# Issuing a tuned attention and highway-FFN kernel in the order of a list schedule, with PSUM banks moved from scores to transposes and PV

## The chip, the cores and the metric

One core of one Trainium2 chip. The metric is device microseconds of one launch (median of the runs). The kernel before was timed at 243.35 us in three runs ahead of the prediction. Ratios are the mean time of one kernel's fast runs over the mean of the other's fast runs of the same rounds, so they are not quite the ratio of the medians quoted beside them. A run more than 1.5% above the fastest of its kernel is called slow and is left out of them.

## The reference

Sliding-window attention with a linear (ALiBi) bias, then one highway layer over all tokens. Sizes: 8 batches, 8 heads, 576 positions, head width 64, window 128, model width 512; float32 in and out.

```
scores = q @ k.T / 8 - slope[h] * |i - j|        where 0 <= i - j < 128, else -1e9
attn   = softmax(scores);  x = attn @ v           # x as (8 * 576, 512)
H = relu(x @ w_h);  T = sigmoid(x @ w_t + b_t)
out = T * H + (1 - T) * x
```

## The kernel before

Batches are handled in four *pairs*. A pair has two row stages of eight heads, so the program has 64 *units* (pair, stage, head). A unit is: scores on TensorE (PE; its weight loads are shown apart, as PEld), exponential on ScalarE (ACT), mask multiply on VectorE (DVE), PV matmuls (`attn @ v`) on PE, and normalisation on DVE. A pair's q and k are first transposed on PE, ten groups a pair, each copied out of PSUM, the memory that TensorE writes to, by DVE or ACT. After eight units their 512-wide rows go through the FFN in four or five *blocks*: transpose, H and T matmuls, tanh on ACT, then `0.5*tanh + 0.5` on GpSimd (POOL; I call this the gate arithmetic), the gate multiply on DVE, the output add on POOL, and a store issued by SyncE. All loads of q, k, v and weights are issued by POOL and convert float32 to bfloat16 on the way; the last 64 of the 576 positions of q and k come by loads of their own, the *tail loads*.

In the traces of this case an engine does not pass an instruction that has to wait (VectorE stood 11.36 us at one, below), so the order of the program counts. It is emitted by a hand-written loop:

```python
ps_sc = ...(name="ps_sc", bufs=2)   # a score buffer holds 128x1024 float32
ps_tr = ...(bufs=1); ps_av = ...(bufs=1); ps_a = ...(bufs=1); ps_z = ...(bufs=1)
...
for u in range(NU + 2):
    m, s, h = unit(u)
    if u < NU:
        if u < len(first): transposes(0, *first[u])      # pair 0
        soft(u)                                          # exponential of unit u
        ...                                              # loads of pair m + 1 at r = u % 16 < 9
        if u + 1 < NU: scores(u + 1)                     # straight behind it
    if 1 <= u <= NU: mask(u - 1)
    ...                                                  # half of this slot's FFN steps
    if 2 <= u:
        pv(u - 2); norm(u - 2)
    ...                                                  # the other half
    if u < NU and m + 1 < ND:
        r = u % (2 * H)
        if r >= 5 and r - 5 < len(TRS):
            transposes(m + 1, *TRS[r - 5])               # next pair, from unit 5 on
```

The bias of T is added by a matmul of one row: `nc.tensor.matmul(out=pz, lhsT=ones1, rhs=bT, ...)` with `ones1` of 1x128 and `bT` of 1x512.

The softmax here doesn't subtract the row's maximum and nothing guards it: scores larger than these inputs give would overflow.

## Time and profile before

| part of the span | from, to (us) | length |
|---|---|---|
| start of the program to unit 0's exponential | 0 to 10.7 | 10.7 |
| units 0 to 15 | 10.7 to 73.7 | 63.0 |
| units 16 to 31 (pair 1) | 73.7 to 125.1 | 51.4 |
| units 32 to 47 (pair 2) | 125.1 to 179.1 | 54.0 |
| units 48 to 63 (pair 3, up to the last exponential) | 179.1 to 216.8 | 37.7 |
| tail | 216.8 to 245.3 | 28.5 |

How to read it: the start of each unit's exponential is a mile post that every version of the kernel has, so stages of two versions can be laid side by side. The lines behind the table are in the prediction. FFN work of one stage runs beside the units of later stages, so a stage's length also depends on how much FFN work was put off into it. The profiled run took 247.06 us, 2.0% above the fastest of this kernel (242.29) and so slow by the rule above: the stages together are some 4 us longer here than in a fast run, and a difference of 1 us in one of them says nothing.

### The profile page before, as it was taken

Reading aid. Unit: us, or ns where it says so; the run is one execution under the profiler, and the core shown is the slowest. Engines: PE = TensorE matmul, PEld = TensorE weight load, DVE = VectorE, ACT = ScalarE, POOL = GpSimd, SP = SyncE. Lnnn points to the kernel's source line nnn. Section 1 sums busy time; section 2 is a strip of 40 time slices with the busy share of each in tenths; the row PEclk is TensorE's granted clock in tenths of the full one; section 3 lists DMA queues with packets and bytes.
Section 4 is the critical chain, followed back from the end, with each engine's and each line's share of the span. In section 5 each row is a group of like instructions: output and inputs, shape, how many; then the busy total and the mean of one; then the engine's idle time right before and its main releaser. Section 6 shows DMA issues by size and latency. Waiting matters only on the chain.

```text
span 245.3 us, 5032 instructions
## 1 busy us (share of the span) xinstructions
PE 177.5 (72%) x2004; PEld 96.5 (39%) x2004; DVE 142.1 (58%) x339; ACT 126.3 (51%) x157; POOL 119.1 (49%) x139
## 2 busy tenths in 40 slices
PE   1355702498898777868887986888887997887980
PEld 1133402376553334445533343455443344533430
DVE  4169501364677656565786575365786586785340
ACT  2324610185665756447675645646656766562440
POOL 8987733300245876531257784412233356223572
PEclk9999965556999999799999798879999999999996
DMA  5999999995019999930159999530113223122243
GB/s 61 135 191 190 167 129 198 143 108 12 6 41 157 217 199 163 104 73 17 45 81 217 208 155 127 67 74 0 45 43 77 54 56 78 43 63 69 52 112 92
DMA packets 70199, 24.97 MB, mean 102 GB/s; under 512 B 48160, under 2 KB 65568, under 8 KB 70176
## 3 DMA queue, kind: packets, MB, share of 16 engines
q0 software_dynamic: 63392, 15.21, 80.5%
q1 hardware_dynamic: 6784, 9.45, 15.3%
q8 instruction: 15, 0.25, 0.4%
q14 instruction: 8, 0.07, 0.1%
HBM read 30.41 MB, written 9.44 MB: 162 GB/s over the span
## 4 chain that ended last, share of the span: by engine, by line
POOL 34%; issue 25%; DMA 16%; DVE 9%; PE 8%; ACT 3%; SPq 2%; POOLq 1%; ACTq 0%
POOL ot L368 16%; DMA kl<-in_k_dram 8%; POOL tt L359 8%; DMA out_dram<-ot 5%; DVE uu L364 5%; POOL va L102 4%; DMA ql<-in_q_dram 3%; PE pt L197 3%; SPq L380 2%; PE av L290 2%; DVE m L167 1%; POOL ktl L93 1%; PE sc L254 1%; ACT xt L332 1%; POOL kl L73 1%
## 5 line engine op out<-in xcount | busy, mean ns | idle before, releaser
L264 ACT ACTIVATE pt<-sc,bias 128x1024 bf16<-128x1024 f32 x64 | 71.0, 1118 | 0.7 <-PE sc L254 0.7
L359 POOL TENSOR_SCALAR tt<-tt 128x512 f16<-128x512 f16 x36 | 22.2, 618 | 85.8 <-ACT tt L358 77.7
L368 POOL TENSOR_TENSOR ot<-uu,x 128x512 f32<-128x512 bf16 x36 | 44.5, 1235 | 19.6 <-DVE uu L364 16.3
L273 DVE TENSOR_TENSOR pt<-pt,m 128x1024 bf16<-128x1024 bf16 x64 | 52.2, 816 | 0.0
L364 DVE TENSOR_TENSOR uu<-uu,tt 128x512 bf16<-128x512 bf16 x36 | 15.3, 426 | 52.4 <-POOL tt L359 52.4
L290 PE MATMUL av<-va,pt 128*128 128x65 bf16 (+1 forms) x576 | 32.7, 205 | 13.8 <-DVE x L316 12.1
L358 ACT ACTIVATE tt<-pz 128x512 f16<-128x512 f32 x36 | 21.5, 597 | 39.3 <-PE pz L355 38.1
L340 PE MATMUL pa<-wH,xt 128*128 128x512 bf16 x144 | 39.8, 401 | 1.3 <-ACT xt L332 0.8
L353 PE MATMUL pz<-wT,xt 128*128 128x512 bf16 x144 | 38.9, 394 | 0.0
L290 PEld LDWEIGHTS <-pt 128*128 128x128 bf16 (+1 forms) x576 | 24.7, 105 | 33.7 <-DVE x L316 22.2
L332 ACT COPY xt<-pt 128x512 bf16<-128x512 bf16 x36 | 21.1, 586 | 31.2 <-PE pt L326 31.0
L209 ACT COPY kt<-pt 128x1024 bf16<-128x1024 bf16 x16 | 16.2, 1012 | 39.4 <-PE pt L197 39.4
L254 PE MATMUL sc<-qt,kt 64*128 64x256 bf16 (+2 forms) x384 | 29.6, 260 | 7.2 <-ACT kt L209 4.4
L316 DVE TENSOR_TENSOR x<-av,rd 128x256 bf16<-128x256 f32 (+1 forms) x64 | 29.3, 458 | 6.0 <-POOL ot L368 3.8
L197 PE MATMUL pt<-ident,ql 128*64 128x128 bf16 x256 | 13.3, 255 | 22.5 <-DMA ql<-in_q_dram 13.4
L102 POOL DMA_DIRECT2D va<-in_v_dram x20 | 22.2, 1113 | 12.6 <-DMA kl<-in_k_dram 4.5
L344 DVE SCALAR_TENSOR_TENSOR uu<-pa,x 128x512 bf16<-128x512 f32 x36 | 24.6, 682 | 5.3 <-PE pa L340 5.3
L326 PE MATMUL pt<-ident,x 128*128 128x128 bf16 x144 | 15.2, 228 | 8.4 <-DVE qt L204 4.2
L254 PEld LDWEIGHTS <-kt 64*128 64x128 bf16 x384 | 14.8, 100 | 15.9 <-issue 6.4
L197 PEld LDWEIGHTS <-ql 128*64 128x64 bf16 x256 | 10.6, 131 | 25.4 <-DMA ql<-in_q_dram 19.2
L204 DVE COPY qt<-pt 128x1024 bf16<-128x1024 bf16 x16 | 11.0, 689 | 15.2 <-PE pt L197 15.2
L340 PEld LDWEIGHTS <-xt 128*128 128x128 bf16 x144 | 11.7, 100 | 15.4 <-issue 4.5
(45 smaller groups left out, 129.1 us busy)
## 6 DMA issues: line engine op xcount, KB each, us to landing
out_dram<-ot SPq DMA_DIRECT2D x128, 64.0 KB, 1.7
va<-in_v_dram POOLq DMA_DIRECT2D x16, 256.0 KB, 8.7
ql<-in_q_dram POOLq DMA_DIRECT2D x3, 1024.0 KB, 11.1
kl<-in_k_dram POOLq DMA_DIRECT2D x3, 1024.0 KB, 12.3
out_dram<-ot SPq DMA_DIRECT2D x8, 128.0 KB, 2.4
ql<-in_q_dram POOLq DMA_DIRECT2D x4, 128.0 KB, 4.8
kl<-in_k_dram POOLq DMA_DIRECT2D x4, 128.0 KB, 5.3
ql<-in_q_dram POOLq DMA_DIRECT2D x2, 256.0 KB, 7.2
```

Of the source, the lines that this page charges most:

```text
L102: nc.gpsimd.dma_start(out=VA[i][0:n, c, :, :, 0:D].rearrange("s r h d -> s (r h) d"), in_=v[2 * m : 2 * m + 2, :, c * P : c * P + n, :].re ...
L197: nc.tensor.transpose(out=pt[r * D : (r + 1) * D, hl * 512 + t * P : hl * 512 + (t + 1) * P], in_=L[:, r, 2 * hp + hl, t * D : (t + 1) * D ...
L254: nc.tensor.matmul(out=sc[:, r, off : off + w], lhsT=KT[i][rows, h, j * P : (j + 1) * P], rhs=rhs, start=True, stop=True,)
L264: nc.scalar.activation(out=pt[:], in_=SC.pop(u)[:], func=ACTF.Exp, bias=BIAS[:, h : h + 1], scale=scale,)
L273: nc.vector.tensor_tensor(out=pt[:], in0=pt[:], in1=mk.to_broadcast([P, 2, 512]), op=ALU.mult,)
L290: nc.tensor.matmul(out=av[rows, g, :], lhsT=pt[:, r, off : off + w], rhs=va[:, j, r, h, :], start=n == 0, stop=n == len(terms) - 1,)
L316: nc.vector.tensor_tensor(out=x[:, 0:nb, h * D : (h + 1) * D], in0=av[:, 0:nb, 0:D], in1=rd[:, 0:nb].to_broadcast([P, nb, D]), op=ALU.mult,)
L340: nc.tensor.matmul(out=pa[:], lhsT=xt[:, c, :], rhs=wH[:, c, :], start=c == 0, stop=c == NCK - 1)
L353: nc.tensor.matmul(out=pz[:], lhsT=xt[:, c, :], rhs=wT[:, c, :], start=c == 0, stop=False)
L359: nc.gpsimd.tensor_scalar(out=tt[:], in0=tt[:], scalar1=0.5, scalar2=0.5, op0=ALU.mult, op1=ALU.add)
L364: nc.vector.tensor_tensor(out=uu[:], in0=uu[:], in1=TT.pop((st, b))[:], op=ALU.mult)
L368: nc.gpsimd.tensor_tensor(out=ot[:], in0=UU.pop((st, b))[:], in1=X[st][:, b, :], op=ALU.add)
```

## The change

Its intent: no hand-placed order. The builder makes a graph of pieces (each with an engine, an estimated cost, a priority, what it depends on, and which PSUM buffers it takes and frees), simulates the engines greedily, and emits the pieces in the order of their simulated start. Beside that, PSUM goes from two score buffers to one, which makes room for a second transpose and a second PV buffer (a *bank* below). The first loads are cut in two instead of three parts; the mask tables are halved and built with five broadcast instructions instead of 37; four k copies of pair 0 go from ScalarE to VectorE; some other buffers grow. The diff, cut to its core (`# ...` marks cuts):

```diff
-    ps_sc = ...bufs=2; ps_tr = ...bufs=1; ps_av = ...bufs=1; ps_a, ps_z = ...bufs=1
+    RING = {"sc": 1, "tr": 2, "av": 2, "a": 1, "z": 1}
-    p0 bufs=11, p1 bufs=4, x bufs=2, ot in ft (bufs=3)
+    p0 bufs=12, p1 bufs=5, x bufs=3, ot bufs=4
-    load_qk(0, slice(0, 2)); # ... load_qk(0, slice(2, 4)); load_qk(0, slice(4, 8))
+    # slice(0, 2), then slice(2, 8), q and k apart
-    M0, M1: 5 copies and 32 tensor_scalar of 128x128 or 128x64
+    def c_mask(s):  # copies, and tensor_tensor with a broadcast per-head column
+    # evac/f_xe/f_u/f_th/f_t/f_st: each copy or follow-up is now a piece of its own
-    for u in range(NU + 2): # ... the hand-written loop
+    node("ident", "POOL", 600, -90, c_ident)
+    # ...
+    def ld(key, prio, nbytes, emit, deps=(), cost=850):
+        node(key, "POOL", cost, prio, emit, deps, land=nbytes)
+    # ...
+    ld(("qk", m, w, 0), tl + w * T, qk_b, ..., [("tr", m - 2, w, hp) for hp in range(4)], cost=1200)
+    node(("qkm", u), "PE", (330, 360)[s], tu - 1.3 * T, ..., need, take=["sc"])
+    node(("exp", u), "ACT", 1118, tu - 1.2 * T, ..., [("qkm", u), "cbias"], free=["sc"])
+    node(("z", kb), "PE", 1090, t + 0.5 * dt, ..., take=["z"])
+    node(("t", kb), "POOL", 630, t + 0.6 * dt, lambda kb=kb: f_t(*kb), [("th", kb)])
+    # ...
+    while todo:
+        # per engine: candidates with the earliest possible start; within LOOK = 100 ns the
+        # lowest priority number; of all engines the one that starts first
+        # ...
+        if land:                      # a load
+            dma = max(dma, t + cost) + land / RATE      # 370 bytes a ns
+            when[key] = dma + LAND                      # 2000 ns
+    order.sort(key=lambda o: o[0])
+    for t, key in order:
+        nodes[key][3]()
```

## The prediction

> **What bounds the kernel now.** I read in this order: the page's busy shares and slices, the table of stages, the timeline where TensorE is empty, the waits, the chain, the groups. First the slices of the page, 40 over the span.
>
> ```profile
> PE   1355702498898777868887986888887997887980
> DVE  4169501364677656565786575365786586785340
> ACT  2324610185665756447675645646656766562440
> PEclk9999965556999999799999798879999999999996
> DMA  5999999995019999930159999530113223122243
> ```
>
> TensorE (PE) is the busiest engine, but there is a hole in slices 5 to 7, near 30 to 50 us, while the DMA row is full and PEclk has fallen to half. Afterwards PE sits at seven to nine tenths, no engine at ten.
>
> I cut the span where the softmax exponentials (64 "units": 4 batch pairs x 2 row stages x 8 heads) start: unit 0 at 10.7 us, unit 7 at 49.5, unit 16 at 73.7, unit 32 at 125.1, unit 48 at 179.1, the last at 216.8. The table of windows, with columns as headed:
>
> ```profile
> core 0: us, PE busy (x) PEld busy (x) DVE busy (x) ACT busy (x) POOL busy (x), PEclk, DMA share, GB/s
> 10.70:30.50 19.80, 11.37 (x144) 7.38 (x144) 13.05 (x53) 8.88 (x9) 15.86 (x23) 1.00 1.74 183
> 30.50:49.50 19.00, 4.58 (x66) 3.44 (x64) 3.44 (x8) 2.85 (x5) 6.08 (x6) 0.55 2.44 155
> 49.50:73.70 24.20, 22.05 (x308) 14.65 (x309) 15.62 (x33) 16.27 (x21) 4.50 (x5) 0.79 1.21 41
> 73.70:125.10 51.40, 41.11 (x503) 22.20 (x502) 33.75 (x72) 31.11 (x40) 27.21 (x30) 0.97 0.94 117
> 125.10:179.10 54.00, 44.17 (x503) 23.07 (x502) 33.80 (x72) 31.24 (x41) 26.21 (x29) 0.91 0.89 111
> 179.10:216.80 37.70, 32.24 (x330) 15.61 (x328) 26.82 (x62) 24.89 (x33) 15.64 (x16) 1.00 0.26 63
> 216.80:245.30 28.50, 18.67 (x123) 8.09 (x122) 11.92 (x25) 8.72 (x15) 14.13 (x16) 0.92 0.31 75
> ```
>
> The reader is to see two losses. In 30.5 to 49.5 us only 4.6 of 19 us are PE work. In the two middle batch pairs 16 units take 51 and 54 us with 41 and 44 of PE work, 3.2 to 3.4 us a unit, against 2.5 in the last pair, which has no loads and no q/k transposes to do. The hole, from the timeline:
>
> ```profile
> 30.91 0.68 POOL L93 DMA_DIRECT2D ktl<-in_k_dram  x1 [1.00 <-DMA va<-in_v_dram]
> 34.83 1.15 POOL L102 DMA_DIRECT2D va<-in_v_dram  x1 [3.23 <-DMA va<-in_v_dram]
> 40.52 1.06 PE L197 MATMUL pt<-ident,ql 128*64 128x128 bf16 x16 [9.97 <-DMA ql<-in_q_dram]
> 46.21 1.06 PE L197 MATMUL pt<-ident,kl 128*64 128x128 bf16 x16 [2.38 <-DMA kl<-in_k_dram]
> ```
>
> The source places the transposes of the *next* pair at unit 5. PE works in program order, so it stands until those loads land at 40.5 and 46.2 us, although units 7 to 15 are computable. The losses of the middle, from the waits:
>
> ```profile
> PEld L290 <- DVE x L316: 22.2, 26, 1.5
> PE av L290 <- DVE x L316: 12.1, 22, 1.1
> PE pt L197 <- ACT xt L332: 6.3, 10, 0.7
> PE pt L326 <- DVE qt L204: 4.2, 5, 1.6
> ```
>
> The first two are the single PV bank: the next unit's PV matmuls wait until VectorE has normalised the last one. The others are the single transpose bank. The chain of waits puts 34% on POOL and 25% on issue, but POOL is 49% busy with its largest wait 77.7 us for the tanh, so I read it as a follower of the in-order latency loop, not as the bound.
>
> **What the Trainium skill says.** (1) "TensorE: Matmul & The Clock Gate", What's actually happening: after an idle window of about 3.4 us the array runs at half clock until some 3.4 us of activity. The trace agrees in sign: clock 0.55 in the hole and 0.79 over the 24 us after it. So the hole costs more than its length. (2) Same page, Back-to-back issue gap: a warm 512-column matmul is spaced about 216 ns. The trace: four starting at 180.89 end at 181.93, the last lasting some 0.38, so (1.04-0.38)/3 = 0.22 us; it agrees. (3) "SBUF — State Buffer", Who interferes with whom: a VectorE instruction with two SBUF inputs contends with a GpSimd instruction that reads SBUF, and one fully blocks. The trace agrees: the mask multiply takes 0.68 us alone and 1.23 to 1.27 where it meets POOL's 1.15 us add; its mean is 0.816. The change leaves both operations in place.
>
> **Part by part.**
>
> *Floor of PE per pair.* From start-to-start times at full clock in the timeline: scores 0.32 us, PV 0.30 or 0.50, a q or k transpose group 0.57 (tails 0.42), FFN block: x transposes 0.27, H matmuls 0.9, T matmuls with bias 1.29 (pz from 173.66 to the next PE work at 174.95; the builder's table believes 1.09). For 16 units, 9 blocks, 10 transpose groups: 16x0.32 + 8x0.8 + 8x0.57 + 2x0.42 + 9x2.46 = 39 us. VectorE: masks 16x0.7, norms 8x0.62 + 8x0.69, q copies 4x0.69+0.42, FFN 9x1.05 = 34, and 3 of port contention: 37. ScalarE: 16x1.12 + 9x1.19 + 4.6 = 33. So PE, closely followed by VectorE, could do a pair in 39 us against 51 and 54.
>
> *Reordering, start to unit 16 (73.7 us now).* Transposes of the next pair now come when the scheduler's DMA model (370 GB/s of source bytes, 2 us landing) has them. The trace agrees with that rate: about 15 MB of float32 were in by 46 us, started at 2, so 350. First pair plus weights are 9.2 MB, landed near 29 us; next q at about 37 and k at 42. Units 0 and 1 start near 11 to 13 as now. The larger load of heads 2 to 7 (1.6 MB each for q and k) lands later than the two-head one does now: units 2 onward at about 20 instead of 18. Then 2.2 us a unit (VectorE also takes three k copies of 1.2), so unit 7 at about 34 instead of 49.5. Units 8 to 15 with four FFN blocks (10 us of PE), ten transpose groups (5.4) and their own 0.97 each come to 23 us of PE, or 2.9 a unit: unit 16 at 58. Gain 15 to 16.
>
> *Banks and order, middle.* PE idle is 10 us in each middle pair. Two PV and two transpose banks and the interleaving should take over half: 44.5 each instead of 51.4 and 54.0, 88% of that at the floor of 39. Gain 16.
>
> *Last pair, units 48 to 63.* Its PE floor without transposes is 33.6 for 16 units, 31.5 for the 15 intervals; now 37.7. The single score buffer adds a round trip: 1.12 exponential, 0.45 to 0.6 scores, two handoffs of 0.1, about 1.9 a unit at best, plus whatever PE piece is in the way. I give it 36.5. Gain 1.
>
> *Tail after the last exponential, 28.5 us.* About seven FFN blocks of 2.46, then tanh, POOL, VectorE, POOL, store. Nothing shortens these; 27.5. Gain 1.
>
> *Mask set-up.* 32 small multiplies (3.5+1.6 us) and copies become five broadcast operations of the builder's estimated 3.4 us; they delay the first mask (21.2 us now). It is ahead of the first-stage pile-up, so 1 to 3 us, counted above.
>
> Sum: 58 + 44.5 + 44.5 + 36.5 + 27.5 = 211 us of span. The timed median before is 243.35 against this profile's 245.3, so 2 less: **209 us**, ratio 0.86.
>
> **Rivals.**
> (a) *The one score buffer becomes the bound.* Scores must wait for the previous exponential, and PE pieces of 0.9 to 1.3 us cannot be broken off. For: PE's own wait on the exponential is 2.4 us in three places even with two buffers. Against: 1.9 is under the 2.44 of PE's floor. If it wins, 2.9 a unit in all middle and last pairs: 46, 46, 43, giving 220.
> (b) *POOL stops in the load queue.* In the trace an issue waits until the DMA eight issues before has landed (3.2 and 4.5 us). The builder charges a load 0.9 to 1.6 us and knows no such limit, so it may place all loads of the first three pairs ahead of the first gate arithmetic on POOL. VectorE, in order, then stands at the first gate multiply until about 48 us. I expect 3 us of this, already inside unit 16 at 58; at worst 10, giving 217.
> (c) *The schedule fits.* If order and banks bring a pair to 41 and unit 16 to 53, it gives 198.
> (d) *The static order is wrong on the chip*, as durations differ (1.29 for 1.09, masks of 1.24, cold clock), so in-order engines wait for each other as now. Then only the hole is gained: 228.
>
> **Range and chances.** The centre is 209; (c) gives the low end, (a) or (b) the high: **196 to 222**. Only (d) together with (b) comes near 238. Faster by over 2%: 0.95, within 2%: 0.04, slower: 0.01.
>
> **What would show it.** Right if: no PE wait over 4 us on a q or k load between 20 and 50 us; unit 7's exponential by 36 us, unit 16's at 54 to 63; the two middle pairs at 42 to 48 us each with PE at 85% or more; waits of PV on the norm multiply down from 12 us to under 4; clock from 20 to 70 us above 0.85. Wrong if: waits of scores on the exponential exceed 15 us in total, (a); VectorE's gate multiply or POOL waits over 8 us on a load near 40 to 50 us, (b); the tail is far from 27 us; or the middle pairs stay at 50.

## The result

The changed kernel takes 212.93 us (210.85 to 215.28, four runs) against 245.18 us of the kernel before in the same rounds (four runs, 242.29 to 251.03). The ratio is 0.8741 with a 95% interval of 0.8579 to 0.8903: faster, 3.9 us from the predicted 209 and inside the range. The profiled run has a span of 212.3 us.

The slices of the page, for the changed kernel:

```profile
PE   0547765995079679999999999999999999997940
DVE  5626767570094164898886988897789979873550
ACT  2340355657023544889878868877878778824420
PEclk9999999999555855999999999999999999999995
DMA  5599999999999999994223999322223333324244
```

There is still a hole, now in the tenth and eleventh slices (48 to 58 us, a slice is 5.3 us), and the clock falls to half behind it until some 85 us. After that the TensorE row is nines to the tail, which the kernel before never had. The table of windows, cut at the starts of units 0, 7, 14, 16, 32, 48 and 63 (columns as in the prediction):

```profile
10.80:33.10 22.30, 14.04 (x176) 9.45 (x175) 13.40 (x24) 7.81 (x8) 14.74 (x18) 1.00 1.94 177
33.10:49.70 16.60, 14.95 (x220) 9.49 (x222) 9.97 (x23) 10.29 (x12) 6.34 (x7) 1.00 2.00 173
49.70:71.40 21.70, 12.89 (x151) 7.84 (x145) 8.66 (x18) 7.70 (x10) 11.71 (x13) 0.61 2.47 175
71.40:114.40 43.00, 40.12 (x474) 21.08 (x474) 30.71 (x67) 30.48 (x39) 24.67 (x26) 0.88 1.14 129
114.40:152.70 38.30, 38.30 (x502) 21.11 (x503) 32.65 (x72) 30.90 (x40) 21.97 (x24) 1.00 0.75 95
152.70:184.40 31.70, 31.51 (x336) 16.09 (x334) 28.20 (x63) 25.56 (x33) 16.31 (x18) 1.00 0.30 72
184.40:212.30 27.90, 18.35 (x123) 8.15 (x121) 12.24 (x24) 8.26 (x14) 14.25 (x16) 0.91 0.34 81
```

Laid beside the table of before: unit 16 starts at 71.4 instead of 73.7, pair 1 takes 43.0 instead of 51.4, pair 2 38.3 instead of 54.0, pair 3 31.7 instead of 37.7, the tail 27.9 instead of 28.5. So of the 33 us between the two profiles (some 31 by the ratio of fast runs) only 2.3 came from the start and 30 from the three pairs. Between units 14 and 16 there are 21.7 us with 12.9 of TensorE work at a clock of 0.61.

What stands in the new hole, from the timeline of POOL and VectorE (start, duration, engine, line, operation; in brackets the idle time before and what ended it):

```profile
49.44 1.16 POOL L75 DMA_DIRECT2D ql<-in_q_dram  x1 [0.27 <-PE pz L383]
50.59 1.15 POOL L75 DMA_DIRECT2D kl<-in_k_dram  x1
56.74 0.68 POOL L95 DMA_DIRECT2D ktl<-in_k_dram  x1 [2.08 <-DMA va<-in_v_dram]
57.45 0.63 POOL L394 TENSOR_SCALAR tt<-tt 128x512 f16<-128x512 f16 x1
58.12 0.42 DVE L399 TENSOR_TENSOR uu<-uu,tt 128x512 bf16<-128x512 bf16 x1 [11.36 <-POOL tt L394]
72.33 1.36 POOL L95 DMA_DIRECT2D ktl<-in_k_dram  x2 [5.96 <-DMA kl<-in_k_dram]
73.70 0.64 POOL L394 TENSOR_SCALAR tt<-tt 128x512 f16<-128x512 f16 x1
```

The first tanh had ended at 42.7 us. Its gate arithmetic ran at 57.45, because in POOL's program order two v loads of pair 1 (out at 47.2, after a wait of 4.2 us) and the q, k and tail loads of *pair 2* stand in front of it, and in this trace the issue of a load waits until the load eight issues earlier has landed. The k load issued at 50.59 shows this: the tail load eight issues behind it goes out at 72.33, right after its landing, with a gate arithmetic behind that again. VectorE, in order, stood 11.4 us at the gate multiply, and with it masks, normalisations and TensorE. From the waits (engine, tile and line; what ended the wait; us in total, times, longest us), first one of before that the prediction passed over, then three of the changed kernel:

```profile
DVE uu L364 <- POOL tt L359: 52.4, 36, 2.9
DVE uu L399 <- POOL tt L394: 16.8, 6, 11.4
PE pt L346 <- DVE x L336: 3.7, 3, 2.7
PE sc L274 <- ACT pt L284: 3.4, 4, 1.3
```

The wait of PV on the normalisation, 12.1 us before, has no line any more; only the x transposes of the FFN wait on it, 3.7 us, of which 2.7 at 75.5 us behind the second late gate arithmetic. The one score buffer costs TensorE 3.4 us of waits.

The first line is the larger matter in the pairs. In the kernel before VectorE stood at every one of the 36 gate multiplies until POOL had done the gate arithmetic: 14.2, 15.5 and 8.4 us in pairs 1, 2 and 3, and normalisations and copies behind it. The hand-written loop emits that multiply one FFN step behind its T matmuls. In the changed kernel the same wait is 3.3, 0.2 and 0.6 us.

### The profile page after: what moved, and what is told of

Its sections match the earlier page's. It is cut to its first block, busy times and chain, and to the rows that moved or that the text cites. A ratio compares the mean times of both kernels' runs of the same rounds, so it can differ in the third digit from the quotient of the medians.

```text
span 212.3 us, 5013 instructions
## 1 busy us (share of the span) xinstructions
PE 173.5 (82%) x2004; PEld 95.4 (45%) x2004; DVE 142.4 (67%) x308; ACT 124.2 (58%) x161; POOL 119.5 (56%) x137
## 3 DMA queue, kind: packets, MB, share of 16 engines
q1 hardware_dynamic: 6784, 9.45, 18.1%
## 4 chain that ended last, share of the span: by engine, by line
PE 57%; DMA 25%; POOL 10%; issue 2%; ACT 2%; DVE 1%; POOLq 1%; SPq 0%; ACTq 0%; DVEq 0%
DMA kl<-in_k_dram 19%; PE pz L381 14%; PE pa L364 13%; PE sc L274 8%; PE av L310 8%; DMA va<-in_v_dram 6%; PE pz L383 5%; PE pt L210 4%; PE pt L346 4%; POOL va L104 3%; POOL ql L83 2%; POOL kl L83 1%; POOL ot L403 1%; ACT pt L284 1%; POOL tri L142 1%
## 5 line engine op out<-in xcount | busy, mean ns | idle before, releaser
L403 POOL TENSOR_TENSOR ot<-uu,x 128x512 f32<-128x512 bf16 x36 | 45.4, 1262 | 21.6 <-DVE uu L399 18.1
L295 DVE TENSOR_TENSOR pt<-pt,mk 128x1024 bf16<-128x1024 bf16 x64 | 49.1, 769 | 6.0 <-ACT pt L284 5.5
L394 POOL TENSOR_SCALAR tt<-tt 128x512 f16<-128x512 f16 x36 | 23.1, 641 | 37.6 <-ACT tt L390 34.7
L310 PE MATMUL av<-va,pt 128*128 128x65 bf16 (+1 forms) x576 | 33.2, 206 | 9.5 <-DVE pt L295 8.0
L381 PE MATMUL pz<-wT,xt 128*128 128x512 bf16 x144 | 39.8, 401 | 0.2 <-ACT tt L390 0.2
L274 PE MATMUL sc<-qt,kt 64*128 64x256 bf16 (+2 forms) x384 | 28.5, 258 | 5.1 <-ACT pt L284 3.4
L335 DVE RECIPROCAL rd<-av 128x4 f32<-128x4 f32 (+1 forms) x64 | 11.7, 183 | 15.6 <-PE av L310 15.1
L274 PEld LDWEIGHTS <-kt 64*128 64x128 bf16 x384 | 13.7, 98 | 16.2 <-issue 11.5
L381 PEld LDWEIGHTS <-xt 128*128 128x128 bf16 x144 | 12.3, 101 | 14.4 <-issue 4.3
L364 PEld LDWEIGHTS <-xt 128*128 128x128 bf16 x144 | 12.3, 100 | 12.8 <-issue 3.6
L210 PE MATMUL pt<-ident,ql 128*64 128x128 bf16 x256 | 11.8, 244 | 6.9 <-POOL ident L127 5.0
L210 PE MATMUL pt<-ident,kl 128*64 128x128 bf16 x256 | 12.9, 256 | 3.9 <-DMA kl<-in_k_dram 2.2
## 6 DMA issues: line engine op xcount, KB each, us to landing
kl<-in_k_dram POOLq DMA_DIRECT2D x3, 1024.0 KB, 18.1
qtl<-in_q_dram POOLq DMA_DIRECT2D x8, 64.0 KB, 16.5
```

The costliest lines, as they stand in the source:

```text
L210: nc.tensor.transpose(out=pt[r * D : (r + 1) * D, hl * 512 + t * P : hl * 512 + (t + 1) * P], in_=L[:, r, 2 * hp + hl, t * D : (t + 1) * D ...
L274: nc.tensor.matmul(out=sc[:, r, off : off + w], lhsT=KT[i][rows, h, j * P : (j + 1) * P], rhs=rhs, start=True, stop=True,)
L295: nc.vector.tensor_tensor(out=o, in0=o, in1=mk, op=ALU.mult)
L310: nc.tensor.matmul(out=av[rows, g, :], lhsT=pt[:, r, off : off + w], rhs=va[:, j, r, h, :], start=n == 0, stop=n == len(terms) - 1,)
L364: nc.tensor.matmul(out=pa[:], lhsT=xt[:, c, :], rhs=wH[:, c, :], start=c == 0, stop=c == NCK - 1)
L381: nc.tensor.matmul(out=pz[:], lhsT=xt[:, c, :], rhs=wT[:, c, :], start=c == 0, stop=False)
```

## The experiments

Theory 1 (from the trace): POOL's program order makes the new hole. Its rivals: the transfers themselves are too slow, or the time is lost on other engines. Question 2: how much of the gain is the order (with its side edits), how much the banks? Theory 3: from some 80 us on TensorE is the bound. Twelve kernels were run, each correct and timed in three rounds beside the kernel before; the table lists all of them, the texts after it their edits.

| run | median us | ratio (95%) | unit 16 at |
|---|---|---|---|
| changed kernel | 212.93 | 0.8741 (0.8579 to 0.8903) | 71.4 |
| late loads | 205.33 | 0.8442 (0.8359 to 0.8526) | 62.1 |
| gate arithmetic on VectorE | 205.69 | 0.8474 (0.8395 to 0.8553) | 58.2 |
| schedule knows the limit of eight | 216.12 | 0.8922 (0.8859 to 0.8986) | 67.3 |
| new order, old banks | 213.61 | 0.8811 (0.8763 to 0.8859) | 68.0 |
| old order, new banks | 324.81 | none given; before 246.03 | 84.9 |
| old order, later transposes | 245.93 | 0.9925 (0.9792 to 1.0058) | 69.3 |
| split first loads | 212.47 | 0.8637 (0.8532 to 0.8741) | 70.3 |
| bias matmul on 128 rows | 206.76 | 0.8438 (0.8368 to 0.8508) | 70.6 |
| late loads, old banks | 212.20 | 0.8669 (0.8570 to 0.8768) | 60.7 |
| late loads, 128-row bias | 201.66 | 0.8246 (0.8138 to 0.8354) | 60.2 |
| the same, and later v loads | 196.69 | 0.8094 (0.7984 to 0.8205) | 57.7 |
| the same, and split loads | 201.11 | 0.8244 (0.8149 to 0.8338) | 61.8 |

The profiled runs of the late loads, the split loads and the late loads with old banks were the slowest of their kernels by 1.5 to 2.3%, so unit 16's time there may be up to 2% late; their medians and ratios are not affected. The granted clock differs between runs too: from 20 to 45 us it was 0.59 to 0.73 in the profiles of five versions (late loads, gate arithmetic on VectorE, limit of eight, and two of those put together) and 1.00 in the others, with much the same TensorE work before it. So a difference of a few us at unit 16 proves nothing by itself.

### Late loads

```diff
-                   [("tr", m - 2, w, hp) for hp in range(4)], cost=1200)
+                   [("tr", m - 2, w, hp) for hp in range(4)] + [("o", (2 * m - 4, 3))], cost=1200)
-                   [("tr", m - 2, w, 4)], cost=1450)
+                   [("tr", m - 2, w, 4), ("o", (2 * m - 4, 3))], cost=1450)
```

`("o", (st, b))` is the output add of block b of FFN stage st. Only the order changes; the bytes and the kinds of instruction are the same.

> The q, k and tail loads of pairs 2 and 3 are ordered after the last output add of the first FFN stage of the pair two before; nothing else is told to move. Theory (POOL's program order: loads that must wait for a landing eight issues back stand in front of the gate arithmetic, VectorE stands in order at the gate multiply): the first gate arithmetic runs near 50 us instead of 57.5, the 11.4 us wait of the gate multiply shrinks to under 4, unit 16 starts near 60 instead of 71.4, time 200 to 204, ratio to before about 0.83. Rival (the transfers themselves are too slow: q, k and v of pair 1 are not there before): unit 16 stays at 68 or later, time 210 to 215.

Measured: 205.33 us, 0.8442 against 0.8741, so about 7 us less. From the timeline, the first gate arithmetic and its multiply:

```profile
49.06 0.64 POOL L394 TENSOR_SCALAR tt<-tt 128x512 f16<-128x512 f16 x1
49.73 0.43 DVE L399 TENSOR_TENSOR uu<-uu,tt 128x512 bf16<-128x512 bf16 x1 [3.38 <-POOL tt L394]
```

It runs at 49.06 instead of 57.45, and the wait falls from 11.4 to 3.4 us, both as theory 1 says, while the transfers of pair 1 are untouched. The time is a little above the 200 to 204 that I gave. Unit 16 starts 9.3 us earlier, but pair 2 takes 43.0 us instead of 38.3: there TensorE now waits 2.7 us on q and k, which come later, and its clock is 0.96 instead of 1.00.

### Gate arithmetic on VectorE

```diff
-        nc.gpsimd.tensor_scalar(out=tt[:], ...)
+        eng = nc.vector if st < 2 else nc.gpsimd
+        eng.tensor_scalar(out=tt[:], ...)
-                node(("t", kb), "POOL", 630, ...
+                node(("t", kb), *(("DVE", 300) if st < 2 else ("POOL", 630)), ...
```

> Only the gate arithmetic (0.5*tanh+0.5) of the first two FFN stages goes to VectorE; the loads keep their place. Theory: the gate multiply no longer waits for POOL; the output adds still stand behind loads, so the three gate buffers fill and about half of the gain of moving the loads comes: unit 16 near 64, time 204 to 209. Rival (transfers too slow): no change, 210 to 215.

Measured: 205.69 us. The loads kept their place and still the time fell by 7 us, so the transfers were not what held up unit 16. Two edits that share only this, that the gate arithmetic no longer stands behind the loads of pair 2, give the same gain, with intervals just clear of the change's (0.8526 and 0.8553 at most, against 0.8579 at least): theory 1 holds. Unit 16 starts at 58.2, sooner than I expected, but pair 1 takes 48.5 us instead of 43.0. What stays there is the output add, which also stands behind loads: VectorE waited 10.6 us in three places for gate buffers that POOL's add frees.

### The schedule knows the limit of eight

```diff
+        if land and len(landed) > 8 - NDMA[key]:
+            t = max(t, landed[NDMA[key] - 9] + SYNC)
         return t
...
             when[key] = dma + LAND
+            landed += [when[key]] * NDMA[key]
```

`NDMA` is how many DMA issues a load piece has (one or two).

> The list schedule is told that a load issue cannot start before the landing of the DMA eight issues earlier, so it may put gate arithmetic in front of a blocked load by itself. Theory: as for late loads or better, since every load is covered: unit 16 at 57 to 61, time 198 to 204. Rival (transfers too slow): 210 to 215 and unit 16 at 68 or later.

Measured: 216.12 us, no gain over the change and perhaps a loss (the two intervals overlap); my expectation failed. Its first gate arithmetic does run at 42.76, as intended. But the schedule is greedy: it takes what can start first, and a tail load, two issues, must wait for a later landing than a single v load. So it put the k tails of pair 1, which every unit from 16 on needs, behind five v loads, the gate arithmetic and the output add of the first blocks, and a q load of pair 2. From the timelines of POOL and PE:

```profile
50.16 1.40 POOL L95 DMA_DIRECT2D ktl<-in_k_dram  x2
65.31 0.39 PE L219 MATMUL pt<-ident,ktl 64*128 64x64 bf16 x8 [1.56 <-DMA ktl<-in_k_dram]
```

In the changed kernel these two tail loads go out at 31.4 and 33.2 us. No unit's exponential starts between 53.0 and 67.3 us. So here a true model of the limit was worth nothing, as the choice ignores who needs the load.

### New order with old banks, old order with new banks

```diff
-    RING = {"sc": 1, "tr": 2, "av": 2, "a": 1, "z": 1}
+    RING = {"sc": 2, "tr": 1, "av": 1, "a": 1, "z": 1}
```

> The changed kernel with the banks of before (two score buffers, one transpose bank, one PV bank), order recomputed by the same schedule. If the banks give the gain of the middle, pairs go from 43 and 38 us back to 48 to 52 and the time to 230 to 238. If the order gives it, pairs stay at 40 to 45 and the time at 212 to 220. My expectation: in between, 222, with waits of PV on the norm near 10 us again.

Measured: 213.61 us, no difference that the intervals can tell from the change. My 222 and the waits of 10 us were wrong. With one PV bank and one transpose bank, as before, the wait of PV on the normalisation is now

```profile
PE av L310 <- DVE x L336: 1.9, 4, 0.7
```

against 12.1 us in the old order, and TensorE's waits for the one transpose bank are 0.8 us in pairs 1 and 2 together, against 12.8. So those waits did not come from the bank count alone: VectorE came late to the normalisations and copies. Its wait at the gate multiply, 3.4, 0.0 and 1.1 us in the three pairs here, is the likely cause; no run changes that multiply's place alone, so this is argued from the traces.

The reverse, in the kernel before:

```diff
-    ps_sc ... bufs=2, ps_tr ... bufs=1, ps_av ... bufs=1
+    ps_sc ... bufs=1, ps_tr ... bufs=2, ps_av ... bufs=2
```

> The kernel before in its old hand-written order, only with the banks of the change (one score buffer, two transpose banks, two PV banks). If banks carry part of the gain: the 12 us in which TensorE waits for the norm go, and the time falls to 230 to 238. If, as the run with the old banks under the new order says, the order carries it: 240 to 250, as the hand-written order puts the PV of a unit directly behind its norm anyway and the single score buffer may cost a little.

Measured: 324.81 us against 246.03, a third slower, which none of my numbers had. The waits point to why:

```profile
PE sc L254 <- ACT pt L264: 84.5, 54, 2.1
```

The old loop emits the scores of unit u+1 directly behind the exponential of unit u, so with one buffer TensorE waits out each exponential, with all its other work queued behind. In the list order other TensorE pieces stand in between, and the same wait is 3.4 us. The single score buffer is therefore affordable only with the new order.

### Late loads with old banks

The edits of the late loads and of the old banks together.

> The run with late loads (205 us) with the old banks (two score buffers, one transpose, one PV bank) under the recomputed order. With the late loads the start is alike in both, so this shows what the banks are worth by themselves. From the stage times of the old-bank run (pairs 43.8, 41.6, 34.2 and tail 30.7 us against 43.0, 38.3, 31.7 and 27.9): 7 to 9 us slower than with the new banks, 212 to 214. Rival (banks worth nothing under the new order, as the equal totals of 213 say): 204 to 207.

The stage times quoted there were misread by one unit: I had counted one exponential twice. The right ones for the new order with old banks are 38.7, 43.3 and 33.4 us for the pairs and 28.4 for the tail. Measured: 212.20 us, 0.8669 against 0.8442 of the late loads with new banks; the intervals do not meet. So with the hole cured the banks are worth 2.3% of the time before, about 5.5 us; by the two intervals the truth may lie 3 us to either side. In the change as it was made this is hidden, because that run's start was shorter (unit 16 at 68.0 instead of 71.4).

### Old order with later transposes

```diff
-                if r >= 5 and r - 5 < len(TRS):
-                    transposes(m + 1, *TRS[r - 5])
+                if m: now = TRS[r - 5 : r - 4] if r >= 5 else []
+                else: now = TRS[2 * r - 22 : 2 * r - 20] if r >= 11 else []
+                for w, hp in now: transposes(m + 1, w, hp)
```

> The kernel before with the transposes of pair 1 placed in units 11 to 15 (two a unit) instead of 5 to 14. Theory of the prediction (the hole at 30 to 49 us is TensorE standing in order at loads not yet there): no TensorE wait over 5 us on a q or k load, unit 7 at 32 to 35 us; how much of it reaches the end: if nothing else takes its place, 12 to 15 us (time 230); if POOL's load queue takes its place as in the changed kernel, 2 to 6 us (time 238 to 241) with a VectorE wait on the gate arithmetic of over 8 us near 45 to 58 us. I expect the second.

Measured: 245.93 us against 246.03. Unit 7 starts at 33.3 instead of 49.5, so the transposes did make the hole of the kernel before; yet unit 16 starts at 69.3 and nothing of it reaches the end that the interval can tell from zero. Neither of my two times (230; 238 to 241) came. VectorE's gate multiply waited 8.8 us in two places between 40 and 70 us, but before both of them POOL was free and waited for the tanh (2.1 and 9.0 us; its last v loads were out by 47.1, the first gate arithmetic ran at 49.2). So POOL's load queue is not what took the hole's place here. In the trace the tanh waits for TensorE, TensorE for the one transpose bank, and the copy that frees the bank stands behind the gate multiply on VectorE; no run tests this loop by itself.

### Split first loads

```diff
-        ld(("qk", 0, w, 1), -60 + w, 3 * qk_b / 4, ... load_qk(0, slice(2, 8), (w,)), cost=1600)
+        ld(("qk", 0, w, 1), -62 + w, qk_b / 4, ... load_qk(0, slice(2, 4), (w,)), cost=1450)
+        ld(("qk", 0, w, 2), -60 + w, qk_b / 2, ... load_qk(0, slice(4, 8), (w,)), cost=1450)
```

> The changed kernel with the large first loads (heads 2 to 7) split as before (heads 2 and 3, then 4 to 7). Unit 2 starts at 18 to 19.5 us instead of 21.8. Theory (the end of the start stage is set by POOL's load queue near 50 to 72 us, not by unit 2): the time stays within 1% of 213. Rival (the start of unit 2 carries through): 210 or less.

Measured: unit 2 at 18.1 us instead of 21.8, unit 16 at 70.3, the time 212.47. The wait at the gate multiply is still 9.3 us. The larger loads of the change cost 3.7 us at unit 2 and nothing measurable at the end (0.8637 against 0.8741, intervals overlapping).

### Bias matmul on 128 rows

```diff
-    ones1 = cp.tile([1, P], BF16, name="ones1");  bT = cp.tile([1, DM], BF16, name="bT")
+    ones1 = cp.tile([P, P], BF16, name="ones1");  bT = cp.tile([P, DM], BF16, name="bT")
         nc.vector.memset(ones1[:], 1.0)
+        nc.vector.memset(bT[:], 0.0)
-            nc.gpsimd.dma_start(out=bT[:], in_=...)
+            nc.gpsimd.dma_start(out=bT[0:1, :], in_=...)
```

> The changed kernel with the bias matmul of the T product on 128 rows (ones 128x128, bias in row 0 of a zeroed 128-row tile) instead of one row: the same 512 columns, so the same streaming time. TensorE's weight load of that matmul waited 0.45 us each of the 36 times (16.5 us in all). Theory: the wait comes from the one-row weight load not being pulled ahead of the matmuls before it; with 128 rows the wait goes and a T product takes 1.1 instead of 1.3 us. As TensorE is the bound from 85 us on, the time falls by 36 x 0.2 = 5 to 7 us, to 206 to 208. Rival 1 (wait stays, it has another cause): 212 to 214. Rival 2 (TensorE is not the bound): wait goes, time stays.

Measured: 206.76 us, as expected. The group of weight loads of this matmul (count, busy us, mean ns, idle before and what ended it), first in the changed kernel:

```profile
L383 PEld LDWEIGHTS <-ones 1*128 1x128 bf16 x36 | 3.3, 91 | 16.5 <-issue 16.5
```

and with 128 rows:

```profile
L384 PEld LDWEIGHTS <-ones 128*128 128x128 bf16 x36 | 3.6, 101 | 4.6 <-issue 0.6
```

All idle time before these loads goes from 16.5 to 4.6 us, and the part that nothing in the profile explains ("issue") from 16.5 to 0.6. The matmul itself lasts 403 ns with one row and 393 with 128, but from the start of a T product to the next piece on TensorE the timelines have a median of 1.29 us with one row and 1.09 with 128; the order of the pieces is the same. Unit 16 is no earlier (70.6), but pair 1 takes 41.5 instead of 43.0, pair 2 36.9 instead of 38.3, pair 3 30.3 instead of 31.7 and the tail 26.6 instead of 27.9. TensorE time was taken away in every stage and every stage after unit 16 got shorter: theory 3 holds there.

### The versions put together

Late loads and 128-row bias:

> Late loads and the 128-row bias matmul together. They act in different stages (start; TensorE from 80 us on), so the gains of 8 and 6 should add: 198 to 200. If the start's gain is partly what TensorE catches up later, 201 to 204.

Measured: 201.66 us, at the lower edge of my second case: the two gains nearly add (0.8442 and 0.8438 alone, 0.8246 together, where 0.8139 would be the full sum).

The v loads later as well:

```diff
-                   [("pv", 2 * H * (m - 1) - 1), ("pv", 2 * H * (m - 1) - 2)], cost=1150)
+                   [("pv", 2 * H * (m - 1) - 1), ("pv", 2 * H * (m - 1) - 2)]
+                   + ([("t", (2 * m - 2, 0))] if c > 1 else []), cost=1150)
```

> As before, and the last three v loads of a pair also after the first gate arithmetic of the stage two earlier. With late loads POOL still stood 4.1 us at a v load before the first gate arithmetic (49.06 us) and VectorE 3.4 us behind it. Theory: that wait goes, 1 to 3 us less than the last run, 196 to 199. Rival: v arrives later and PV waits on it, 200 or more.

Measured: **196.69 us, 0.8094, the fastest version**, 19% below the kernel before. Its fast runs lie about 5 us below those of the last version, more than the 1 to 3 expected. Its first gate arithmetic runs at 43.05 and unit 16 starts at 57.7. Its slices:

```profile
PE   0537676699989987879998988699999999988930
PEclk9999999999999999999999999999999999999985
```

TensorE no longer has a hole, and in this run its clock stays full up to the tail; the other runs of this version have mean clocks of 0.949 to 0.978 against its 0.984, so the full clock is in part luck. The late loads now have a price: TensorE waits 4.9 us on q and k in pairs 1 and 2, and pair 2 takes 40.8 us instead of the 36.9 of the 128-row bias alone.

With the split first loads added (the diff above):

> As before, and the first loads split as in the kernel before. With POOL's queue out of the way the earlier unit 2 (18.1 instead of 21.8 us, measured) may now carry through: 194 to 198. If the arrival of pair 1 (q and k at 42 to 47 us) sets the end of the start stage: no change.

Measured: 201.11 us: slower than the last version in every run: unit 2 at 16.7, but unit 16 at 61.8 and pair 2 at 43.8, and three stretches of half clock before the tail. Every edit of the graph gives a new order of all pieces, so a local gain can be lost elsewhere. Which piece costs it here stays open.

## Why the prediction was right, and where its steps were not

The total was right because two errors of opposite sign met, which was luck. By its own sum (predicted, then measured): start to unit 16, 58 and 71.4; pair 1, 44.5 and 43.0; pair 2, 44.5 and 38.3; pair 3, 36.5 and 31.7; tail, 27.5 and 27.9. Together 211 and 212.3.

- **The start was mis-sized by 13 us.** The mechanism was on the page as rival (b), with the limit of eight read off the trace, but it was given 3 us, 10 at worst. The wrong step is "until about 48 us": I followed the queue to the landing of pair 1's k and took POOL to be free after it, though the same paragraph says that the loads of three pairs may stand in front. The loads of pair 2 did, and POOL reached the gate arithmetic at 57.45. The late loads and the gate arithmetic on VectorE, each about 7 us faster in the end, show this cause: with the gate arithmetic out of POOL's queue unit 16 starts at 58.2, where the sum had 58. One reading in that sum was also off: the loads had moved some 14 MB of float32 by 46 us (7.07 MB of bfloat16 in the trace of before), not 15, and q and k of pair 1 landed at 41.6 and 46.9 us in the changed kernel, not at 37 and 42.
- **The hole of the kernel before had the cause that was given** (transposes of the next pair, placed too early), but the 15 to 16 us expected from filling it were not there. The run with later transposes filled it and gained nothing that could be measured. A hole is worth only what the next limit leaves of it.
- **The pairs were mis-sized the other way.** The floor from start-to-start times was right: 39 us a pair, and pair 2 took 38.3. The failed term is "88% of that at the floor": with the list order pair 2 reached all of it. The Trainium skill, "Perfetto Trace Analysis", Identifying the Most-Contended Engine, warns that the busy share of matmuls is no good measure of how close TensorE is to its roofline. This case agrees only in part: pair 2 of the kernel before was 82% busy, which leaves 10 us, while the spacings said 54.0 - 39 = 15 and 15.7 came. But its clock there was 0.91, so some 10 us ran at half speed, which can account for up to 5 of the 6 us by which the busy time exceeds the later 38.3. The 128-row bias confirmed that TensorE was the bound. The section that the prediction quotes for 216 ns, Back-to-back issue gap, gives that figure for an isolated matmul and about 131 ns for a stream of weight loads and matmuls; the 0.22 us measured here, in such a stream, speaks against the second.
- **The waits of the middle were misread.** The prediction put PV's waits on the normalisation down to the single PV bank and others to the single transpose bank. With the same banks in the new order they fall from 12.1 to 1.9 us and from 12.8 to 0.8. It did not weigh VectorE's 52.4 us at the gate multiply, which the page showed.
- **Banks and order.** The prediction credited both together. The runs part them: order and side edits without the banks 0.8811, banks alone a third slower, and the banks about 5.5 us once the hole is cured.
- **Rival (a), the score buffer**, was rightly rejected for this order (3.4 us of waits, under the 15 named as its sign), but in the old order it is the largest wait of TensorE (84.5 us).
- **The cold clock** went with the holes: 0.55 in the old one, 0.61 in the new one. It outlasted them: in the kernel before it was 0.50 from 49.5 to 59.6 us, with TensorE 9.7 of 10.1 us busy, so three times the 3.4 us that the prediction takes from the skill. It also fell in other places, and not in every version (see the note under the table of runs). The prediction's "above 0.85 from 20 to 70 us" was just missed, at 0.84.
- **Signs given in advance:** unit 7 by 36 us (33.1, right); unit 16 at 54 to 63 (71.4, wrong); no TensorE wait over 4 us on a q or k load from 20 to 50 us (right); middle pairs at 42 to 48 us (43.0, right, and 38.3, better than that); PV waits on the norm under 4 us (right); the VectorE wait over 8 us near 40 to 50 as the sign of (b) (11.4 us, from 46.8 to 58.1, met); tail near 27 (27.9, right).

## What to carry to other kernels

On engines that work in program order, ask of every queue that mixes transfers with arithmetic what a blocked transfer will hold up; put a prefetch behind the short work that others wait for, but not so far behind that it misses its own user. Take the floor of the busiest engine from start-to-start spacings of its pieces at full clock: a good order can reach it. A wait for a buffer need not mean too few buffers; ask first why the engine that frees it comes late. Buffer counts and issue order are one decision: the single score buffer here was nearly free in one order and cost a third of the time in the other.

## What the Trainium skill lacked or had wrong

- "TensorE: Matmul & The Clock Gate", The mechanism, says in one sentence that a weight load overlaps matmuls in flight only when its row group differs; another sentence there also lets it run ahead into the background weight buffer. The runs agree with the second: before the 36 loads of 128 rows, behind 128-row matmuls, the idle time was 4.6 us in all. Before one-row loads in the same place it was 16.5, and the page has no word on this cost of a one-row matmul: 0.20 us each by the spacings (1.29 against 1.09 us).
- No page that I read has the number of loads that POOL can have in flight before an issue waits for a landing. In these traces it was eight (issue at 72.33 behind the landing of the load of 50.59). The packed traces show the issues taking eight semaphores in turn, which fits a limit of the program; no run changes it, so whether the chip has one is not shown.
